# More buffers and longer leads for the half-precision parts of an attention and expert block

## The chip, the cores and the metric

The kernel runs on one core of one Trainium2 chip. The metric is the device time of one execution in microseconds (us), as the median of several runs. The core's engines are TensorE (PE, with its weight loads PEld), VectorE (DVE), ScalarE (ACT), GpSimd (POOL) and SyncE (SP). Nearly every DMA of this kernel is issued from SP, whose queue works in order: what waits there holds everything behind it.

## What is computed

```python
# x: 2048 tokens x 448 features
def _A_ref(x, wqkv, wo):                     # 16 heads of 28
    q, k, v = ...                            # of x @ wqkv
    p = softmax(q @ k.T * 28 ** -0.5)
    return (p @ v).reshape(...) @ wo

def _B_ref(x, w_q, k1, k2, u, v):            # 4096 experts in a 64 x 64 grid, 16 heads
    q1, q2 = halves of x @ w_q
    s1, s2 = q1 @ k1.T, q2 @ k2.T            # 64 scores each
    ...                                      # best 8 of each, best 8 of their 64 sums
    g = softmax(top_s)
    act = gelu(x . u[top_e])
    return sum(g * act * v[top_e])

h = x + _A_ref(layernorm(x), A_wqkv, A_wo)
return h + _B_ref(layernorm(h), B_w_q, B_k1, B_k2, B_u, B_v)
```

## The kernel before

A first part makes q, k and v, and stores them in DRAM. Then comes attention in 256 steps, called units here: one step is one block of 128 keys for four heads and 512 queries. It makes the scores S (line 526, PE), their exponentials P (line 530, ACT, two activations a step) and the sums A (line 552, PE). The keys and values are loaded again every four steps (`load_kv`, tiles `kS` and `V`). After every 64 steps a block of 512 tokens is done. `project` then turns it into the input of the second half: PE waits there for VectorE's `oh` and `xn`, VectorE for ScalarE. `search` scores the experts and picks the best eight. After attention, from about 1017 us on, the expert sums run; the change does not touch them.

All this is written out as generators, and `weave` puts their steps into one order: an entry (generator, n, lo, hi) spreads n steps over lo to hi, counted in attention steps. There are two weaves, one over steps 0 to 60 and one over the other 197, whose count starts again at 0. Within an engine the instructions stand in that order and run in it.

The expert tables u and v and the folded query weights are needed as half-precision parts: a table of fp32 rows is scaled and written as a high and a low fp16 plane (three planes for v). Three kinds of generators do it:

- `tops(S, ...)` loads a table once to find its largest magnitude; `S.see` is a VectorE reduction (line 139). It runs for u in the first weave (steps 1 to 25) and for v in the second (27 to 50).
- `S.share()` makes the scale from it, the same on all partitions.
- `part(S, src, dst, ...)` loads a block into a tile `raw`, makes the planes in a tile `hl`, and stores them in DRAM. For the folded weights (`parts_of_folded`, 16 parts, steps 5 to 27 of the second weave) VectorE makes them (lines 159 and 993), for u (`parts_of_up`, 14 parts in the first weave, 18 in steps 4 to 50 of the second) and for v (`parts_of_down`) GpSimd does (lines 988 to 990, and 995 for the third plane). `pipeline(..., 1)` starts one part per step, so that the steps of several parts overlap.

Before, a part loads in its first step, computes in its second and stores in its third. `raw` and `hl` have two buffers each, and the folded parts and those of u share them. `tops` has two buffers of 1024 columns of its own. A tile's instructions wait until the buffer that it takes has been read to the end by its last user; for `hl` this is the landing of the store.

Of the kernel before, what the change touches and what calls it, by code (L numbers as in the profile page):

```python
# [29 lines left out]
LS = 2.0 ** 11  # L30
# [28 lines left out]
def block(ctx: ExitStack, tc: tile.TileContext, x, wqk, wv, wo, wq, k12, uT, v, cst, out):  # L59
# [98 lines left out]
    def times(dst, src, c):  # L158
        nc.vector.tensor_scalar(dst, src, c, None, op0=OP.mult)  # L159
# [146 lines left out]
        STEPS = 3 * H  # L306


    US, VS, WS = Scale(0, 16), Scale(1, 16), Scale(2, H)

    fp = ExitStack()
    raw_p = fp.enter_context(tc.tile_pool(name="raw", bufs=2, reuse_waits="tile"))
# [285 lines left out]
    def project(b, offset=5, room=None):  # L598

        X[b] = XH, XL = bx.tile([128, 4, 512], F16, name="XHb"), bx.tile([128, 3, 512], F16, name="XLb")  # L600

        def place(j, name, tag, bufs):
            return room[name][j % len(room[name])] if room else w2.tile([128, 512], F32, name=name, tag=tag, bufs=bufs)

        def tile_of(j):
            r = 512 * b + 128 * j
            c = slice(128 * j, 128 * j + 128)
            xt = place(j, "xt", "xt", 2)[:, :D]
            nc.sync.dma_start(xt, x[r:r + 128])
            of = transposed(ob[b][:, j])  # L610
            oh = w2.tile([128, 4, 128], FR, name="oh2", bufs=1)
            ol = w2.tile([128, 3, 128], FR, name="ol2", bufs=1)
            if room:
                nc.scalar.activation(oh, of, AF.Copy)
            else:
                kept = w2.tile([128, 4, 128], F32, name="of", bufs=1)
                nc.scalar.activation(kept, of, AF.Copy)
                of = kept
            yield
            if not room:  # L620
                nc.vector.tensor_copy(oh, of)
            lows(oh, ol, of)
            yield
            if not room:
                yield
            pa = P[0].tile([128, 512], F32, name="M")
            mm_all(pa[:, :D], products(lambda t: oh[:, t], lambda t: ol[:, t], lambda t: woh[:, t], lambda t: wol[:, t]))
            at = place(j, "at", "xn", 1)[:, :D]
            nc.scalar.activation(at, pa[:, :D], AF.Copy)
            yield  # L630
            nc.vector.tensor_tensor(xt, at, xt, op=OP.add)
            nc.sync.dma_start(h_d[4 * b + j], xt)
            mean, rstd = moments(w2, xt)
            yield
            if not room:
                yield
            xn = w2.tile([128, 512], F32, name="xn2", tag="xn", bufs=1)[:, :D]
            norm(xt, xn, mean, rstd, nc.vector)
            if not room:
                yield  # L640
            xf = transposed(xn)
            if room:
                nc.scalar.activation(XH[:, :, c], xf, AF.Copy)
            else:
                kept = w2.tile([128, 4, 128], F32, name="xf", bufs=1)
                nc.scalar.activation(kept, xf, AF.Copy)
                xf = kept
            yield
            if not room:
                yield  # L650
                nc.vector.tensor_copy(XH[:, :, c], xf)
            lows(XH[:, :, c], XL[:, :, c], xf)
            yield

        yield from pipeline([tile_of(j) for j in range(4)], offset, -1 if room else 1)
        if not room:
            store_X(b)
# [310 lines left out]

    def tops(S, src, cols):

        raw = None
        for k in range(17):
            last = raw
            if k < 16:
                raw = sp.tile([128, 1024], F32, name="tops")
                nc.sync.dma_start(raw[:, :cols], src(2 * k))
            if last is not None:
                S.see(k - 1, last[:, :cols])
            yield

    def part(S, src, dst, cols, planes):
        raw = sp.tile([128, 512], F32, name="raw")
        nc.sync.dma_start(raw[:, :cols], src)
        yield
        hl = sp.tile([128, 3, 512], F16, name="hl")
        r, h = raw[:, :cols], [hl[:, k, :cols] for k in range(planes)]
        if planes == 3 or S is US:
            nc.gpsimd.tensor_scalar(r, r, S.scale, 1.0, op0=OP.mult, op1=OP.mult)
            nc.gpsimd.tensor_copy(h[0], r)
            nc.gpsimd.tensor_tensor(h[1], r, h[0], op=OP.subtract)  # L990
        else:
            times(h[0], r, S.scale)
            nc.vector.scalar_tensor_tensor(h[1], r, S.scale, h[0], op0=OP.mult, op1=OP.subtract)
        if planes == 3:
            nc.gpsimd.tensor_scalar(h[2], h[0], 1.0 / LS, 1.0, op0=OP.mult, op1=OP.mult)
        yield
        nc.sync.dma_start(dst, hl[:, :planes, :cols])
        yield

    def parts_of_up(f0, f1):  # L1000
        return pipeline([part(US, uT[:, f].rearrange("p t e -> p (t e)"), us_d[f], 512, 2) for f in range(f0, f1)], 1)
# [4 lines left out]
    def parts_of_folded():  # L1006
        return pipeline([part(WS, wr_d[h].rearrange("p t c -> p (t c)"),
                              wp_d[h // 4][:, :, h % 4].rearrange("p f t c -> p f (t c)"), 512, 2) for h in range(H)], 1)

    def scales():  # L1010
        times(ugelu, US.floor, 2.0 ** -TOP / XS)
        times(wscale, US.scale, 2.0 ** -17)
        nc.vector.tensor_tensor(oscale, US.floor, VS.floor, op=OP.mult)
        times(oscale, oscale, 2.0 ** -15)
        yield

    with tc.manual_schedule(engines={ET.PE, ET.DVE, ET.Activation, ET.Pool, ET.SP}):
        load_kv(2)
        start = [64 * b + 33 + PAIRED for b in range(3)]
        a = attention({u + 2 * n - 1 for u in start for n in range(16)})  # L1020
        weave((islice(a, 60), 60, 0, 60), (fold[0].run(fold_p, P[0]), Fold.STEPS, 1, 59),
              (tops(US, lambda f: uT[:, f:f + 2].rearrange("p f t e -> p (f t e)"), 1024), 17, 1, 25), (US.share(), 5, 26, 33),
              (parts_of_up(0, 14), 16, 33, 59))
        fp.close()
        bx = ctx.enter_context(tc.tile_pool(name="bx", bufs=1, reuse_waits="tile"))
        bg = ctx.enter_context(tc.tile_pool(name="bg", bufs=1, reuse_waits="tile"))
        bk = ctx.enter_context(tc.tile_pool(name="bk", bufs=1, reuse_waits="tile"))
        iota2 = bg.tile([128, 128, 2], F16)
        ident16 = bg.tile([128, 128], F16)
        sl = [bg.tile([128, 4, 128], F16, name=f"sl{j}") for j in range(4)]  # L1030
        ts4 = bg.tile([128, 4, H, 8], F32)
        for i in range(2):
            nc.vector.tensor_copy(iota2[:, :, i], ct[:, C_IOTA:C_IOTA + 128])
        nc.vector.tensor_copy(ident16, ident)
        places = pp.tile([128, 8, 16 * H], F16, name="places", bufs=1)
        for k in range(8):
            nc.gpsimd.memset(places[:, k], float(k))
        r2 = ExitStack()
        wo_p = r2.enter_context(tc.tile_pool(name="wo_p", bufs=1, reuse_waits="tile"))
        w2 = r2.enter_context(tc.tile_pool(name="w2", bufs=2, reuse_waits="tile"))  # L1040
        woh = wo_p.tile([128, 4, D], FR)
        wol = wo_p.tile([128, 4, D], FR)
        work = [(a, 197, 0, 197), (load_wo(), 5, 0, 8)]
        for b in range(3):
            t = 64 * b + 7
            look = search(b, [(i, j) for g in ((0, 1), (2, 3)) for i in range(4) for j in g])
            work += [(project(b), PROJECT, t, t + PROJECT), (islice(look, 1), 1, t + 10, t + 11)]
            t += 26
            work += [(look, SEARCH, t, t + SEARCH)]
            if b < 2:  # L1050
                work += [(chain(*[pairs_of(j, nc.gpsimd) for j in range(4)]), 4 * PAIRS_POOL, t + 18, t + 82),
                         (places_of(b, nc.scalar), PLACES, t + 82, t + 94)]
            else:
                work += [(pipeline([pairs_of(j, nc.gpsimd) for j in (0, 1)], 6), 6 + PAIRS_POOL, t + 20, 197)]
        work += [(WS.share(), 5, 0, 5), (parts_of_folded(), 18, 5, 27), (parts_of_up(14, 32), 20, 4, 50),
                 (tops(VS, lambda f: v[:, f:f + 2].rearrange("p f d -> p (f d)"), 2 * D), 17, 27, 50), (VS.share(), 5, 51, 56), (scales(), 1, 56, 57),
                 (parts_of_down(0, 14), 16, 58, 110), (parts_of_down(14, 32), 20, 110, 180)]
        weave(*work)
    att.close()
    late.close()  # L1060
# [176 lines left out]
```

## Time and profile before

| | before |
|---|---|
| time, median of 3 runs | 1780.12 us (1779.68 to 1780.82) |
| the profiled execution, its own time | 1786.24 us |
| its span, first to last instruction | 1784.4 us |
| mean granted TensorE clock | 0.958 |
| busy: PE, DVE, ACT, POOL | 90%, 70%, 50%, 23% |
| share of DMA: SP's queue q1 | 52.7% of 16 engines |

The span is 1.8 us shorter than the time of its own execution, and that execution is 6.1 us longer than the median of the others. In the rows of a window the columns are the window, its length, and for each engine its busy time with the number of instructions in brackets; then the granted TensorE clock, the busy share of the DMA engines and the GB/s that they moved. In the waits each row names who waited, for whom, the sum in us, how often and the longest.

### The profile page before, as it was taken

The page shows a single profiled execution, that of the slowest core. Times are in us where ns is not written, and L with a number is a line of the kernel's source. Part 1 is how long each engine was busy: PE and PEld are TensorE (multiplying, and loading weights), DVE is VectorE, ACT ScalarE, POOL GpSimd, SP SyncE. Part 2 cuts the span into 40 slices and gives each one's busy share as a digit, 9 for nine tenths or more (in the row PEclk, how much of TensorE's full clock was granted, in tenths as well). Part 3 has the DMA queues.
Part 4 walks back from the last instruction along what each step waited for, and adds up shares of the span by engine and source line. Part 5 has one row for each costly group of instructions (what it writes and reads, how often), then busy time and mean ns, then how long its engine had stood idle before and what let it go on. Part 6 is the DMA issues. An engine that isn't in the chain of part 4 may idle for free.

```text
span 1784.4 us, 33450 instructions
## 1 busy us (share of the span) xinstructions
PE 1608.8 (90%) x12577; PEld 816.0 (46%) x12577; DVE 1246.3 (70%) x3875; ACT 897.1 (50%) x1272; POOL 417.2 (23%) x514
## 2 busy tenths in 40 slices
PE   7999889953378999999999889899999999999998
PEld 5776334421133344334433356444554555455544
DVE  6655756422237956776767889995999899879932
ACT  3545566842156788768777534323342334433422
POOL 3452117511123167516743510000000000000000
PEclk9999999976689999999999899999999999999999
DMA  8756757544469556655665123444435543454344
GB/s 261 244 186 213 272 187 260 181 158 130 144 208 316 190 179 215 210 173 164 217 216 171 65 90 114 127 139 127 142 108 142 150 130 108 153 148 137 104 141 134
DMA packets 159748, 301.32 MB, mean 169 GB/s; under 512 B 14816, under 2 KB 58976, under 8 KB 159584
## 3 DMA queue, kind: packets, MB, share of 16 engines
q1 hardware_dynamic: 155360, 297.07, 52.7%
q8 instruction: 99, 1.62, 0.4%
q10 hardware_dynamic: 4224, 2.10, 0.4%
q14 instruction: 65, 0.53, 0.1%
HBM read 237.24 MB, written 61.87 MB: 168 GB/s over the span
## 4 chain that ended last, share of the span: by engine, by line
PE 54%; DVE 27%; DMA 12%; issue 2%; POOL 2%; SPq 1%; ACT 1%; DVEq 0%; POOLq 0%
PE acc L1152 13%; PE M L90 9%; PE A L552 8%; PE S L526 7%; PE A L90 7%; PE pq L90 6%; DVE p L932 4%; DVE ti L762 4%; DMA wp<-hl 3%; DMA tops<-in_v_dram 2%; DVE G L953 2%; DVE ti L761 2%; DVE fg L917 2%; DVE pos L789 2%; DMA us<-hl 1%
## 5 line engine op out<-in xcount | busy, mean ns | idle before, releaser
L530 ACT ACTIVATE P<-S 128x1024 f32<-128x1024 f32 x512 | 496.0, 1022 | 143.7 <-PE S L526 142.2
L1152 PE MATMUL acc<-v,w 128*128 128x448 f16 x1536 | 306.4, 353 | 0.7 <-DVE w L1127 0.7
L552 PE MATMUL A<-P,V 128*32 128x512 f32 x2048 | 272.5, 623 | 10.7 <-DVE o L557 10.7
L526 PE MATMUL S<-qS,kS 32*128 32x512 f32 x3072 | 269.0, 435 | 5.2 <-ACT P L530 4.6
L526 PEld LDWEIGHTS S<-qS,kS 32*128 32x128 f32 x3072 | 141.4, 188 | 164.1 <-issue 98.8
L1152 PEld LDWEIGHTS <-w 128*128 128x128 f16 x1536 | 148.7, 98 | 142.9 <-ACT w L1126 1.8
L90 PEld LDWEIGHTS <-u 128*128 128x128 f16 x1408 | 132.8, 98 | 149.2 <-issue 7.2
L1126 ACT ACTIVATE w<-ring 128x512 f16<-128x512 f32 x128 | 80.5, 630 | 209.2 <-PE acc L1152 109.8
L932 DVE TENSOR_TENSOR p<-st,iota 128x2048 f16<-128x2048 f16 x128 | 156.0, 1220 | 9.0 <-PE A L959 5.5
L90 PE MATMUL A<-XHb,u 128*128 128x512 f16 x568 | 135.4, 381 | 4.1 <-DVE G L953 4.0
L90 PE MATMUL M<-w,XHb 128*128 128x512 f16 x512 | 129.0, 382 | 6.9 <-DVE ob L543 3.7
L1127 DVE SCALAR_TENSOR_TENSOR w<-w,ring 128x512 f16<-128x512 f16 x128 | 87.2, 686 | 66.1 <-ACT w L1126 66.1
L1125 DVE SCALAR_TENSOR_TENSOR ring<-ring,wscale,G 128x512 f32<-128x512 f32 x128 | 92.8, 745 | 34.5 <-ACT ring L1111 34.5
L90 PE MATMUL M<-XHb,u 128*128 128x512 f16 x456 | 110.9, 379 | 0.8 <-DVE G L953 0.8
L552 PEld LDWEIGHTS A<-P,V 128*32 128x32 f32 x2048 | 46.3, 110 | 117.2 <-issue 101.0
L761 DVE MAX8 ti<-fresh 128x8 f32<-128x64 f32 x384 | 80.6, 210 | 16.9 <-ACT fresh L739 16.8
L1111 ACT ACTIVATE ring<-A,ugelu 128x512 f32<-128x512 f32 x71 | 48.5, 683 | 85.1 <-PE A L90 85.1
L813 POOL TENSOR_TENSOR sel<-sel,iv 128x256 f16<-128x256 f16 x80 | 54.2, 707 | 153.1 <-DVE sel L809 153.1
L159 DVE TENSOR_SCALAR hl<-raw,scale 128x512 f16<-128x512 f32 x16 | 7.8, 486 | 113.5 <-DMA wp<-hl 112.8
L762 DVE FIND_INDEX8 ti<-ti,fresh 128x8 uint32<-128x64 f32 x384 | 84.2, 219 | 0.0
L1111 ACT ACTIVATE ring<-M,ugelu 128x512 f32<-128x512 f32 x57 | 39.2, 688 | 81.7 <-PE M L90 81.5
L917 DVE TENSOR_TENSOR fg<-f,st 128x2048 f16<-128x2048 f16 x64 | 78.6, 1229 | 0.1
(197 smaller groups left out, 2360.9 us busy)
## 6 DMA issues: line engine op xcount, KB each, us to landing
v<-vs SPq DMA_DIRECT2D x128, 336.0 KB, 2.9
kS<-ks SPq DMA_DIRECT2D x64, 512.0 KB, 4.8
u<-us SPq DMA_DIRECT2D x128, 256.0 KB, 2.7
w<-wp SPq DMA_DIRECT2D x56, 512.0 KB, 5.4
V<-vd SPq DMA_DIRECT2D x64, 256.0 KB, 3.0
wr<-in_wq_dram SPq DMA_DIRECT2D x32, 448.0 KB, 6.1
vs<-hl SPq DMA_DIRECT2D x32, 336.0 KB, 4.0
qS<-qs SPq DMA_DIRECT2D x16, 512.0 KB, 5.8
```

The costliest lines, as they stand in the source:

```text
L90: nc.tensor.matmul(ps, l, r, start=i == 0, stop=i == len(pairs) - 1)
L526: nc.tensor.matmul(S[j // 2][:, j % 2], kS[r, a, 128 * (k % 4):128 * (k % 4) + 128], qS[r, c], start=m == 0, stop=m == 2)
L530: nc.scalar.activation(Pt[:, 2 * i:2 * i + 2], S[i], AF.Exp)
L552: nc.tensor.matmul(O[n][32 * j:32 * j + 32], V[:, k % 4, j], Pt[:, j], start=k == 0, stop=k == NT - 1)
L761: nc.vector.max(t8[:, 4 * i + k], src[:, 64 * k:64 * k + 64])
L762: nc.vector.max_index(i8[:, 4 * i + k], t8[:, 4 * i + k], src[:, 64 * k:64 * k + 64])
L917: nc.vector.tensor_tensor(fg.rearrange("p t k f u -> p t k (f u)"), f1.rearrange("p t f u -> p t (f u)").unsqueeze(2).to_broadcast([128, T ...
L932: newest[0] = nc.vector.tensor_tensor(p1, pairs(0, s, TG, 128), ids(TG, 128), op=OP.is_equal).ins
L1111: nc.scalar.activation(act, p, AF.Gelu_apprx_tanh, scale=ugelu)
L1125: nc.vector.scalar_tensor_tensor(av, av, wscale, of_expert(b, f), op0=OP.mult, op1=OP.mult)
L1127: nc.vector.scalar_tensor_tensor(w[:, 1], w[:, 0], -LS, a, op0=OP.mult, op1=OP.add)
L1152: nc.tensor.matmul(acc[j][:, :D], l, r, start=f == 0 and k == 0, stop=f == 31 and k == 2)
```

## The change

`tops` reads 32 blocks of 512 columns (448 for v) instead of 16 of 1024 (896), each loaded two steps of its generator ahead of its reduction instead of one; the weave gives it 34 steps instead of 17 in the same stretch. Its tiles are now the `raw` of the parts, of which there are six. A part computes two steps after its load and stores two steps after that. Parts of two planes have five buffers (`hl2`), parts of three planes three (`hl3`). The engines that make the planes stay the same. The first loads of `search` move 12 attention steps later, behind the last folded part.

```diff
-    US, VS, WS = Scale(0, 16), Scale(1, 16), Scale(2, H)
+    US, VS, WS = Scale(0, 32), Scale(1, 32), Scale(2, H)
...
     def tops(S, src, cols):
-        raw = None
-        for k in range(17):
-            last = raw
-            if k < 16:
-                raw = sp.tile([128, 1024], F32, name="tops")
-                nc.sync.dma_start(raw[:, :cols], src(2 * k))
-            if last is not None:
-                S.see(k - 1, last[:, :cols])
+        raw = {}
+        for k in range(34):
+            if k < 32:
+                raw[k] = sp.tile([128, 512], F32, name="raw", bufs=6)
+                nc.sync.dma_start(raw[k][:, :cols], src(k))
+            if k >= 2:
+                S.see(k - 2, raw.pop(k - 2)[:, :cols])
             yield
...
     def part(S, src, dst, cols, planes):
-        raw = sp.tile([128, 512], F32, name="raw")
+        raw = sp.tile([128, 512], F32, name="raw", bufs=6)
         nc.sync.dma_start(raw[:, :cols], src)
         yield
-        hl = sp.tile([128, 3, 512], F16, name="hl")
+        yield
+        hl = sp.tile([128, planes, 512], F16, name="hl", tag=f"hl{planes}", bufs=5 if planes == 2 else 3)
...
         yield
-        nc.sync.dma_start(dst, hl[:, :planes, :cols])
+        yield
+        nc.sync.dma_start(dst, hl[:, :, :cols])
         yield
+    PART = 4
...
-              (tops(US, ...), 17, 1, 25), (US.share(), 5, 26, 33),
-              (parts_of_up(0, 14), 16, 33, 59))
+              (tops(US, ...), TOPS, 1, 25), (US.share(), 5, 26, 33),
+              (parts_of_up(0, 14), 14 + PART, 33, 59))
...
-            work += [(project(b), PROJECT, t, t + PROJECT), (islice(look, 1), 1, t + 10, t + 11)]
+            work += [(project(b), PROJECT, t, t + PROJECT), (islice(look, 1), 1, t + 22, t + 23)]
...
-        work += [(WS.share(), 5, 0, 5), (parts_of_folded(), 18, 5, 27), (parts_of_up(14, 32), 20, 4, 50),
-                 (tops(VS, ...), 17, 27, 50), ...
-                 (parts_of_down(0, 14), 16, 58, 110), (parts_of_down(14, 32), 20, 110, 180)]
+        work += [(WS.share(), 5, 0, 5), (parts_of_folded(), H + PART, 5, 27), (parts_of_up(14, 32), 18 + PART, 4, 50),
+                 (tops(VS, ...), TOPS, 27, 50), ...
+                 (parts_of_down(0, 14), 14 + PART, 58, 110), (parts_of_down(14, 32), 18 + PART, 110, 180)]
```

The order on PE and on ACT stays as it was, instruction for instruction. On SP it changes in the stretch of the two passes and of the parts. At the start of the folded parts (second weave, steps 6 to 13) SP's queue stood so before; `wp` is the DRAM tensor of the folded parts, `us` that of u, `wr` the folded weights, and the numbers tell the tiles apart:

```order
L983 DMA raw_27690<-wr2_68 128x512
L997 DMA wp0_82<-hl_27687 256x1x512
L983 DMA raw_27720<-wr3_69 128x512
L997 DMA us14_120<-hl_27642 128x1024
L983 DMA raw_27748<-in_uT_dram 128x512
L997 DMA wp0_82<-hl_27717 256x1x512
L983 DMA raw_27789<-wr4_70 128x512
```

Now it stands so, at the same place:

```order
L984 DMA raw_27730<-wr2_68 128x512
L984 DMA raw_27759<-wr3_69 128x512
L984 DMA raw_27765<-in_uT_dram 128x512
L1000 DMA wp0_82<-hl_27727 256x1x512
L984 DMA raw_27792<-wr4_70 128x512
L1000 DMA wp0_82<-hl_27756 256x1x512
L984 DMA raw_27833<-wr5_71 128x512
```

The store of the first folded part (`hl_27727`) has moved behind the loads of the third and fourth; two parts of each table are loaded beyond the one that is stored. On SP in the first weave, where the pass over u begins, the rows were these (`wr` is here the raw query weight for the fold):

```order
L201 DMA qS<-qs_58 128x2x512
L976 DMA tops<-in_uT_dram 128x1024
L242 DMA wr<-in_wq_dram 128x896 x2
L976 DMA tops<-in_uT_dram 128x1024
L201 DMA kS<-ks_61 128x2x512
```

And they are now:

```order
L201 DMA qS<-qs_58 128x2x512
L975 DMA raw<-in_uT_dram 128x512 x3
L242 DMA wr<-in_wq_dram 128x896 x2
L975 DMA raw<-in_uT_dram 128x512
L201 DMA kS<-ks_61 128x2x512
```

One load of 1024 columns has become up to three of 512 ahead of the same neighbours.

More of the change, by code (lines that the diff above doesn't have):

```diff
@@ L969, in tops @@
     def tops(S, src, cols):
-        raw = None
-        for k in range(17):
-            last = raw
-            if k < 16:
-                raw = sp.tile([128, 1024], F32, name="tops")
-                nc.sync.dma_start(raw[:, :cols], src(2 * k))
-            if last is not None:
-                S.see(k - 1, last[:, :cols])
+        raw = {}
[5 more added lines that the diff above has]
+                S.see(k - 2, raw.pop(k - 2)[:, :cols])
             yield
+    TOPS = 34
     def part(S, src, dst, cols, planes):
-        raw = sp.tile([128, 512], F32, name="raw")
+        raw = sp.tile([128, 512], F32, name="raw", bufs=6)
         nc.sync.dma_start(raw[:, :cols], src)
         yield
-        hl = sp.tile([128, 3, 512], F16, name="hl")
+        yield
+        hl = sp.tile([128, planes, 512], F16, name="hl", tag=f"hl{planes}", bufs=5 if planes == 2 else 3)
         r, h = raw[:, :cols], [hl[:, k, :cols] for k in range(planes)]
-        if planes == 3 or S is US:
+        if S is WS:
+            times(h[0], r, S.scale)
+            nc.vector.scalar_tensor_tensor(h[1], r, S.scale, h[0], op0=OP.mult, op1=OP.subtract)
+        else:
             nc.gpsimd.tensor_scalar(r, r, S.scale, 1.0, op0=OP.mult, op1=OP.mult)
@@ L990, in part @@
             nc.gpsimd.tensor_tensor(h[1], r, h[0], op=OP.subtract)
[L991 to L995, printed above, removed]
+            if planes == 3:
+                nc.gpsimd.tensor_scalar(h[2], h[0], 1.0 / LS, 1.0, op0=OP.mult, op1=OP.mult)
         yield
-        nc.sync.dma_start(dst, hl[:, :planes, :cols])
         yield
+        nc.sync.dma_start(dst, hl[:, :, :cols])
+        yield
+    PART = 4
     def parts_of_up(f0, f1):
@@ L1021, in block @@
         weave((islice(a, 60), 60, 0, 60), (fold[0].run(fold_p, P[0]), Fold.STEPS, 1, 59),
-              (tops(US, lambda f: uT[:, f:f + 2].rearrange("p f t e -> p (f t e)"), 1024), 17, 1, 25), (US.share(), 5, 26, 33),
-              (parts_of_up(0, 14), 16, 33, 59))
+              (tops(US, lambda f: uT[:, f].rearrange("p t e -> p (t e)"), 512), TOPS, 1, 25), (US.share(), 5, 26, 33),
+              (parts_of_up(0, 14), 14 + PART, 33, 59))
         fp.close()
@@ L1054, in block @@
                 work += [(pipeline([pairs_of(j, nc.gpsimd) for j in (0, 1)], 6), 6 + PAIRS_POOL, t + 20, 197)]
-        work += [(WS.share(), 5, 0, 5), (parts_of_folded(), 18, 5, 27), (parts_of_up(14, 32), 20, 4, 50),
-                 (tops(VS, lambda f: v[:, f:f + 2].rearrange("p f d -> p (f d)"), 2 * D), 17, 27, 50), (VS.share(), 5, 51, 56), (scales(), 1, 56, 57),
-                 (parts_of_down(0, 14), 16, 58, 110), (parts_of_down(14, 32), 20, 110, 180)]
+        work += [(WS.share(), 5, 0, 5), (parts_of_folded(), H + PART, 5, 27), (parts_of_up(14, 32), 18 + PART, 4, 50),
+                 (tops(VS, lambda f: v[:, f], D), TOPS, 27, 50), (VS.share(), 5, 51, 56), (scales(), 1, 56, 57),
+                 (parts_of_down(0, 14), 14 + PART, 58, 110), (parts_of_down(14, 32), 18 + PART, 110, 180)]
         weave(*work)
```

## The prediction

> **What bounds the kernel now.** I first read the page's slices, to find where PE, which is busy 90% of the span, is not.
>
> ```profile
> PE   7999889953378999999999889899999999999998
> ```
>
> Slices 9 to 12 (357 to 535 us; a slice is 44.6 us) hold 5, 3, 3 and 7 tenths. Second come the windows around that hole, first those of all engines, then the exponentials alone (line 530, two per attention step).
>
> ```profile
> 154.50:197.10 42.60, 41.11 (x352) 17.85 (x354) 30.40 (x40) 32.50 (x35) 8.43 (x4) 0.96 0.75 262
> 197.10:246.20 49.10, 37.71 (x288) 16.49 (x284) 31.08 (x42) 24.84 (x27) 6.30 (x3) 0.86 0.68 226
> 356.40:520.20 163.80, 75.09 (x568) 35.01 (x571) 40.41 (x81) 53.06 (x61) 30.65 (x40) 0.70 0.46 144
> 520.20:563.50 43.30, 38.50 (x303) 14.48 (x303) 24.37 (x99) 26.23 (x29) 12.33 (x15) 0.93 0.93 320
> 644.60:708.20 63.60, 63.27 (x568) 29.54 (x571) 40.55 (x130) 52.64 (x60) 42.05 (x59) 1.00 0.62 199
> 708.20:744.70 36.50, 35.55 (x303) 13.99 (x304) 26.30 (x149) 26.26 (x30) 18.70 (x26) 1.00 0.73 233
> 540.00:550.00 10.00, 9.27 (x63) 3.29 (x67) 7.28 (x39) 3.81 (x5) 2.50 (x4) 0.83 1.01 376
> ```
>
> ```profile
> 154.50:197.10 42.60, 31.03 (x32) 0.96 0.75 262
> 197.10:246.20 49.10, 23.26 (x24) 0.86 0.68 226
> 356.40:520.20 163.80, 46.43 (x49) 0.70 0.46 144
> 644.60:708.20 63.60, 46.43 (x48) 1.00 0.62 199
> ```
>
> The kernel contains its own control. 356.4:520.2 and 644.6:708.2 are the same 24 attention steps of two blocks, with the same 568 matmuls and the same `project`. The first takes 163.8 us, the second 63.6 with PE busy for 63.27. What the first has more is the folded parts and those of u. Third, the waits in that window (the last row is SP's own queue):
>
> ```profile
> DVE hl L159 <- DMA wp<-hl: 112.8, 15, 16.4
> POOL hl L989 <- DMA us<-hl: 84.2, 8, 14.4
> PEld M L119 <- DVE xn L113: 60.0, 3, 26.5
> SPq L983 <- DVE hl L993: 53.0, 12, 9.1
> ```
>
> VectorE stands 112.8 us before making a folded part until the store of an earlier part has landed; PE stands 60 us for `project`'s `xn`, which is queued behind that on VectorE. Fourth, the chain of waits shows the loop:
>
> ```profile
> 407.73 3.26 DMA wp<-hl
> ...
> 411.12 0.50 DVE hl L159
> ...
> 411.64 0.76 DVE hl L993
> ...
> 412.42 0.33 SPq L983
> ...
> 412.79 3.07 DMA wp<-hl
> ```
>
> A store lands (3.1 to 3.3 us), VectorE makes the planes (0.50 + 0.76), SP, which waited for the raw buffer, issues a load (0.33), only then the next store, and so on: 4.9 us a part, strictly in series, because two `hl` and two `raw` serve both tables. Sixteen folded parts make 78 us of it, and ten parts of u of the same build the rest.
>
> In the first weave there is a smaller hole. Steps 0 to 16 take 42.6 us, 2.66 a step; the next twelve 49.1, 4.09 a step:
>
> ```profile
> 201.14 1.22 DVE L139 TENSOR_REDUCE tops<-tops 128x1 f32<-128x1024 f32 x1 [4.09 <-DMA tops<-in_uT_dram]
> ...
> 206.07 0.71 PE L90 MATMUL M<-wqh,kk 128*128 128x448 f32 x1 [5.16 <-DVE wt L267]
> 221.21 0.44 PE L90 MATMUL M<-wqh,kk 128*128 128x448 f32 x1 [1.15 <-DVE wt L267]
> 234.57 0.71 PE L90 MATMUL M<-wqh,kk 128*128 128x448 f32 x1 [4.96 <-DVE wt L267]
> ```
>
> VectorE waits for a block of u that could not be loaded earlier for want of a third buffer, and PE's fold waits behind it.
>
> **The change part by part.**
>
> *The parts in the second weave.* In steps of the weave, a folded part computes every 22/20 = 1.1 steps, one of u every 46/22 = 2.1. In the built program each compute now takes a buffer whose store stands up to two steps earlier in SP's order (before: in the same step, just ahead), and that store's data were made two or four steps before, so SP need not wait for it. A cycle of three folded parts needs some 1.26 + 0.33 + 3.3 = 4.9 us against 3.3 steps of 2.65 (63.6/24) = 8.7. So the loop opens. What is late next?
>
> - PE: 63.6 us, the twin window.
> - DMA: the bytes stay. The busy share of 0.46 over 163.8 us is 75.3 us of DMA time. The fullest stretch of the table, 520.2:563.5, reached 0.93, so 75.3/0.93 = 81.0 us. This is more than PE's 63.6, so DMA is the next bound.
> - Waits that stay. Four folded parts late in the stretch take a buffer of u whose store stands in SP's order in the same step as their compute. If SP is not ahead, each costs VectorE a store issue and landing, 0.33 + 3.3 us and what SP still has ahead of it, some 4.5: 0 to 18 us in all. I take 8, near the middle, since a stall of VectorE also leaves DMA idle.
>
> So 163.8 becomes 81 + 8 = 89, a gain of 75. The bounds: 100 if PE alone binds, 44 in the second rival below.
>
> *The pass over u.* Its loads may now run up to six reductions ahead instead of two, 1.5 MB instead of 1 MB in flight. I take back the three PE stalls shown: 5.16 + 1.15 + 4.96 = 11.3 us. At best the twelve steps go at 2.66 us, 49.1 - 31.9 = 17.2 (the clock of 0.86 recovers too); at worst nothing. DMA in 154.5:246.2 is 0.75 x 42.6 + 0.68 x 49.1 = 65.3 us busy and does not bind the 80.4 us that are left.
>
> *The pass over v* (second weave, steps 27 to 50). Its lead in bytes hardly changes, the DMA share is at 0.93 there, and its bytes are the same. Its twin 708.2:744.7 takes 36.5 us against 43.3, so 0 to 6.8 are to be won; I take 0.
>
> *More, smaller operations.*
>
> ```profile
> L139 DVE TENSOR_REDUCE tops<-tops 128x1 f32<-128x1024 f32 x16 | 19.3, 1208 | 11.4 <-DMA tops<-in_uT_dram 11.4
> L139 DVE TENSOR_REDUCE tops<-tops 128x1 f32<-128x896 f32 x16 | 17.2, 1078 | 24.0 <-DMA tops<-in_v_dram 24.0
> L139 DVE TENSOR_REDUCE tops<-of 128x1 f32<-128x512 f32 x16 | 10.9, 682 | 23.2 <-ACT of L279 23.2
> ```
>
> 32 reductions of 512 at 0.682 are 21.8 us for 19.3; 32 of 448, about 0.60, 19.1 for 17.2: 4.4 us more on VectorE, and 32 more issues of 0.33 are 10.6 us on SP. VectorE is busy 61 of 92 us and 24 of 43 in these stretches, so I take 0; without that cover it is up to 15.
>
> *Queues passed.* The loads now stand ahead of `kS` and `V` loads that were ahead of them, and six of the v blocks ahead of the GpSimd operation that frees their buffer. SP can stand there up to 2.5 us each, 0 to 15. The keys behind are loaded eight steps (over 20 us) before they are used; I take 0. The stores two steps later have no near reader: `search` reads the folded parts, and its first loads move with them. These are three transfers, now four steps (10.6 us) ahead of the search, which needs two of them first.
>
> ```profile
> tops<-in_uT_dram SPq DMA_DIRECT2D x16, 512.0 KB, 5.1
> raw<-in_uT_dram SPq DMA_DIRECT2D x32, 256.0 KB, 4.3
> tops<-in_v_dram SPq DMA_DIRECT2D x16, 448.0 KB, 5.7
> raw<-in_v_dram SPq DMA_DIRECT2D x32, 224.0 KB, 4.2
> w<-wp SPq DMA_DIRECT2D x56, 512.0 KB, 5.4
> ```
>
> Two `w` at 5.4 just fit if they come one after the other; in three blocks a late one may cost some us each, 0 to 15 in all. I take 0. The parts of v, with three buffers of their own, lie in windows where PE is already busy to 99% (63.27 of 63.60): 0.
>
> *Sum.* 75 + 11.3 = 86 off the span of 1784.4 gives 1698; the execution's own 1786.2 becomes 1700. It stood 6.1 above the median of the runs, 1780.1, so the median should be **1694 us**.
>
> **The rivals.**
>
> *DMA doesn't bind.* [...] 144 GB/s x 163.8 us are 23.6 MB; in 63.6 us that is 371 GB/s, and one stretch of 10 us reached 376. Then PE binds: 100.2 + 17.2 gained, 1663. Against it: 376 held for 10 us only, and with a share of 1.01. "Perfetto Trace Analysis" of the Trainium skill (section Roofline) lets a single core reach about 435 GB/s over its 16 DMA engines; by that these bytes would take an estimated 54 us, and this rival would be the forecast. The row of 376 at a full share speaks against counting on it. Chance 0.10.
>
> *The change does only part of what it says: the buffers still tie the two tables.* SP can't run ahead, because it waits for folded stores and `xt` of the same steps, and every folded part still waits for one issue and landing, 0.33 + 3.2 = 3.5 us, on VectorE: 16 x 3.5 = 56 on top of 63.6 is 120 us, a gain of 44. With the 11.3 of the pass over u this gives 1725. For it: five buffers for two tables is few. Chance 0.14.
>
> *Slower: the halved loads go one at a time.* A load of half the size lands hardly sooner, 4.3 for 5.1 and 4.2 for 5.7. If SP stops between them, at a `V` whose buffer PE still reads or at a `raw` that a part still holds, so that fewer than two blocks are in flight, the pass over u needs 32 x 4.3 = 138 us instead of 91.7 (+46), and that over v 32 x 4.2 = 134 instead of some 83 (23 steps at 43.3/12; +51). Less the 75 of the parts this is +22: 1802. With two or more in flight it is harmless. Against it stand the six buffers and the 0.33 us of an issue. Chance 0.05. The Trainium skill, "DMA: Bandwidth & Descriptors", section Rules for kernel authors, speaks against the change in the same way: many small transfers are to be coalesced, and full bandwidth wants 1 MiB per DMA. By it the halving alone would slow both passes; the rows above agree that a half load saves only 0.8 to 1.5 us, but here the loads can overlap.
>
> *No change that can be measured*, the gain eaten by all the small terms at once: 0.01.
>
> **How the numbers follow.** My forecast, 1675 to 1715 around 1694, gets 0.70; the rivals 0.10, 0.14, 0.05 and 0.01. The range 1670 to 1730 holds the forecast, most of the partial case and the edge of the fast one, and leaves out under 0.2. A measurement of this kernel tells 0.2% (3.6 us) from no change. Faster: 0.70 + 0.10 + 0.14 = 0.94; same 0.01; slower 0.05.
>
> **What would show it.** Right: 24 attention steps after about 345 us in 80 to 100 us, VectorE's wait for `wp<-hl` down from 112.8 to under 20, DMA share there over 0.8, PE's clock back near 1, no PE wait of 5 us in the pass over u. Wrong: VectorE still waiting for `wp<-hl` by 40 us or more, a DMA share at 0.5, or SP waiting long for GpSimd in front of raw loads, with PE waiting for `V` or `kS`.

## The result, and the profile after

The changed kernel takes 1703.43 us in the median of four runs (1696.69 to 1704.53), beside 1780.47 for the kernel before on the same chip: a ratio of 0.9554, with an interval of 0.9525 to 0.9584, or 77.0 us less. (The ratios here are worked out from all runs; the two medians alone would give 0.9567.) The profiled execution of it took 1696.69 us with a span of 1694.9. That is 89.5 us below the span of before, more than the medians differ, since this execution is 6.7 us under its own median and the profiled one of before was 6.1 over its. Only profiled executions have stages, so stages are compared with stages below, and times with times.

The page's slices of PE and of its granted clock have lost the hole (a slice is 42.4 us here):

```profile
PE   6999898987899999999998899899999999999999
PEclk9999999998999999999999999999999999999999
```

These are the windows of all engines. The first two are steps 0 to 16 and 16 to 28 of the first weave, the third is the 24 steps with the folded parts, the fourth the twelve steps behind, and the last the twin of the third. Steps are counted here, and below wherever a step number goes with a measured stretch, from the start of attention through both weaves; so the 24 steps are 68 to 92, the twelve behind them 92 to 104, and the twin 132 to 156. Only the places to which parts of u are moved below (30 to 120 and the like) are counted as in the weave's table, within the second weave:

```profile
153.30:198.60 45.30, 41.15 (x353) 17.82 (x354) 30.49 (x48) 32.58 (x35) 8.46 (x4) 0.96 0.78 250
198.60:240.90 42.30, 35.49 (x288) 15.64 (x288) 31.38 (x50) 24.74 (x28) 6.31 (x3) 0.92 0.77 257
349.60:432.20 82.60, 68.32 (x568) 31.44 (x572) 50.01 (x83) 53.02 (x61) 36.95 (x44) 0.92 0.85 281
432.20:473.50 41.30, 37.02 (x303) 14.45 (x299) 24.21 (x107) 26.23 (x30) 14.81 (x18) 0.96 0.98 345
554.90:619.60 64.70, 63.38 (x568) 29.61 (x572) 41.35 (x130) 52.66 (x60) 41.33 (x59) 1.00 0.60 181
```

The 24 steps went from 163.8 to 82.6 us: 81.2 of the 89.5. Steps 0 to 28 of the first weave together gave 4.1 (91.7 to 87.6), the twelve steps after the folded parts 2.0, and all the rest 2.2. These are the waits in the 24 steps:

```profile
DVE hl L159 <- DMA us<-hl: 14.5, 4, 5.0
DVE hl L159 <- DMA wp<-hl: 5.9, 2, 4.3
PEld M L119 <- DVE xn L113: 8.1, 2, 5.4
```

VectorE's 112.8 us for `wp<-hl` are 5.9, and PE's 60.0 for `xn` are 8.1. The longest wait is a new one: four times VectorE stands for the store of a part of u. The chain of waits shows one of them:

```profile
386.69 4.86 DMA us<-hl
...
391.68 0.72 DVE hl L159
...
393.09 0.51 DVE xn L113
...
397.79 4.63 DMA wp<-hl
402.41 0.49 DVE hl L159
```

The folded part waits for the buffer of u, `xn` is queued behind it on VectorE, and PE waits for `xn`, as before, but no longer at every part. In the 24 steps PE itself stands five times, always for VectorE, 14.3 us in all: 9.7 us of it (4.45, 1.69 and 3.54) come after the first and the third of the four stalls, while PE works on through the second and the last (3.11 and 4.38).

### The profile page after: what moved, and what is told of

It reads as the page before. It is cut to its first block, busy times and chain, and to the rows that moved or that the text cites. A ratio compares the mean times of both kernels' runs of the same rounds, so it can differ in the third digit from the quotient of the medians.

```text
span 1694.9 us, 33544 instructions
## 1 busy us (share of the span) xinstructions
PE 1598.7 (94%) x12577; PEld 811.4 (48%) x12577; DVE 1254.8 (74%) x3907; ACT 896.7 (53%) x1272; POOL 421.1 (25%) x514
## 4 chain that ended last, share of the span: by engine, by line
PE 62%; DVE 24%; DMA 8%; issue 2%; POOL 1%; ACT 1%; SPq 0%; DVEq 0%; POOLq 0%; ACTq 0%
PE acc L1157 15%; PE M L90 10%; PE A L90 9%; PE A L552 9%; PE S L526 9%; PE pq L90 6%; DVE p L932 4%; DVE ti L762 2%; DVE G L953 2%; DMA raw<-in_uT_dram 2%; DVE fg L917 2%; DVE pos L789 2%; DMA raw<-in_v_dram 1%; DVE ti L761 1%; PE A L959 1%
## 5 line engine op out<-in xcount | busy, mean ns | idle before, releaser
L552 PE MATMUL A<-P,V 128*32 128x512 f32 x2048 | 267.8, 613 | 3.4 <-DVE o L557 3.4
L90 PEld LDWEIGHTS <-XHb 128*128 128x128 f16 x512 | 45.4, 98 | 72.5 <-issue 21.3
```

Source lines behind the costliest of these rows:

```text
L90: nc.tensor.matmul(ps, l, r, start=i == 0, stop=i == len(pairs) - 1)
L552: nc.tensor.matmul(O[n][32 * j:32 * j + 32], V[:, k % 4, j], Pt[:, j], start=k == 0, stop=k == NT - 1)
```

## The experiments

**Which half of the change?** The passes were put back (with five `raw` buffers and narrower tiles for three planes, so that all fits), and then the passes were changed alone, with six buffers of their own.

```diff
# e1_parts_alone: the changed kernel, passes as before
-  raw = sp.tile([128, 512], F32, name="raw", bufs=6)
+  raw = sp.tile([128, 512], F32, name="raw", bufs=5)
+  # tops(), Scale(0, 16), Scale(1, 16), 17 steps as before
# e2_pass_alone: the kernel before, with
+  # tops() of 32 blocks, two ahead
+  raw[k] = sp.tile([128, 512], F32, name="tops", bufs=6)
```

> The parts as changed (leads of two steps, five buffers for two planes), the passes as before (two buffers of 1024 columns, one step ahead; raw has five buffers here, since six do not fit beside them). If the hole was the loop of store, planes and load on two shared buffers, this alone gives nearly all: the 24 attention steps of the first block in 80 to 90 us (163.8 before, 82.6 changed), a time of 1703 to 1715. If the deeper loads of the passes carry a good part of the gain, it stays above 1725.

> The passes as changed (32 blocks of 512 columns, two ahead, six buffers of their own), the parts as before. If the gain is the parts', the first block keeps its 160 us or so and the time falls by 4 to 12 us, to 1768 to 1776, by the first 28 attention steps alone (91.7 us before, 87.6 changed). If halved loads hurt, it is 1785 or more.

The parts alone took 1708.8 us, a ratio of 0.9593 (0.9558 to 0.9627). The passes alone took 1780.53 beside 1781.36, a ratio of 0.9995 (0.9977 to 1.0012). So the parts carry nearly all of the gain, and the passes none that can be measured; the 4 to 12 us that were expected of them did not come. The windows of the 24 steps and VectorE's largest wait there, first of the parts alone, then of the passes alone:

```profile
352.10:436.60 84.50, 70.90 (x568) 32.60 (x572) 44.32 (x81) 52.92 (x60) 35.70 (x43) 0.88 0.83 267
...
DVE hl L159 <- DMA us<-hl: 21.3, 6, 5.5
```

```profile
350.10:514.70 164.60, 77.38 (x568) 36.47 (x572) 41.05 (x82) 53.08 (x60) 30.57 (x40) 0.70 0.47 143
...
DVE hl L159 <- DMA wp<-hl: 113.8, 15, 16.5
```

**Which of the two buffers?** Each was given to the kernel before, alone.

```diff
# e8_raw6: the kernel before, with
-        raw = sp.tile([128, 512], F32, name="raw")
+        raw = sp.tile([128, 512], F32, name="raw", bufs=6)
# e9_hl5: the kernel before, with
-        hl = sp.tile([128, 3, 512], F16, name="hl")
+        hl = sp.tile([128, 3, 512], F16, name="hl", bufs=5)
```

> The kernel before with one edit: six raw buffers for the parts. In the loop SP waits at each raw load for the planes of the part before, and only then issues the store. If the raw buffers close the loop, this alone brings the first block from 163.8 us to 85 to 110 us and the time to 1705 to 1730. If the planes' buffers do, VectorE waits for wp<-hl as long as before (over 80 us), the block stays over 140 us and the time over 1755.

> The kernel before with the other edit alone: five buffers for the planes. If the planes' buffers close the loop, the block goes to 85 to 110 us and the time to 1705 to 1730, with no wait for wp<-hl left. If the raw buffers do as well, SP still waits for planes at each raw load, VectorE now for raw<-wr instead of wp<-hl, the block stays over 120 us and the time over 1735.

They took 1718.97 and 1718.29 us, ratios of 0.964 (0.9614 to 0.9666) and 0.964 (0.9615 to 0.9665): either alone gives four fifths of what the change gives (3.6% of 4.5%). The 24 steps of `raw` alone and of `hl` alone, each with VectorE's largest wait:

```profile
353.30:453.10 99.80, 71.46 (x568) 33.13 (x572) 43.97 (x81) 53.05 (x61) 30.62 (x40) 0.86 0.73 234
...
DVE hl L159 <- DMA wp<-hl: 36.8, 12, 8.9
```

```profile
353.20:450.20 97.00, 72.47 (x568) 33.02 (x572) 42.75 (x81) 52.97 (x60) 31.93 (x40) 0.84 0.75 241
...
DVE hl L159 <- DMA raw<-wr: 45.0, 13, 7.4
```

The loop of the prediction ran through both buffers: a store's landing frees `hl`, the making of planes frees `raw`, and a load refills it, with one SP queue between them. Taking either buffer out of it opens it. What is left is a wait of VectorE for a landing at most of the 16 parts: that of a store where `hl` stays at two (36.8/12 = 3.1 us in the mean), that of a load where `raw` does (45.0/13 = 3.5 us).

**Are the longer leads needed?** The buffers were kept, and a part was given its old steps.

```diff
# e3_old_leads: the changed kernel, part() with
         nc.sync.dma_start(raw[:, :cols], src)
         yield
-        yield
         hl = ...
         ...
         yield
-        yield
         nc.sync.dma_start(dst, hl[:, :, :cols])
-    PART = 4
+    PART = 2
```

> All as changed, but a part computes one step after its load and stores one step after that, as before: only the buffers are more. If the buffers alone break the loop, the first block takes 80 to 95 us and the time is 1700 to 1715. If the leads are needed too (SP waiting at each store for planes just made, VectorE at each part for a load just issued), it takes 100 to 135 us and the time is 1720 to 1755, with VectorE waiting for raw<-wr and SP for hl.

It took 1703.57 us, a ratio of 0.9568 (0.9537 to 0.9599): no different from the whole change. In the windows of the 24 and the next twelve steps and in VectorE's waits one loss stands for another:

```profile
353.30:432.70 79.40, 70.05 (x570) 32.61 (x572) 48.66 (x82) 52.99 (x60) 34.18 (x40) 0.89 0.84 275
432.70:479.00 46.30, 38.82 (x303) 14.86 (x301) 24.72 (x108) 26.28 (x30) 13.05 (x16) 0.93 0.94 333
...
DVE hl L159 <- DMA raw<-wr: 20.3, 7, 4.5
```

The store of u is no longer waited for, since it stands earlier in SP's order; the load of the folded part is, since it has one step less. The 24 steps are 3.2 us shorter, the next twelve 5.0 longer.

**Does DMA bind what is left?** The prediction held DMA to be the next bound at 81 us. If so, more buffers can't help.

```diff
# e4_hl7: the changed kernel, with
-  bufs=5 if planes == 2 else 3
+  bufs=7 if planes == 2 else 3
```

> All as changed, with seven buffers instead of five for parts of two planes. If the four waits of VectorE for us<-hl (14.5 us) and what PE loses behind them are what holds the first block at 82.6 us, they go and it takes 66 to 74 us; time 1688 to 1696. If DMA binds there, as the prediction's 81.0 us had it, the waits go but the block stays at 79 to 83 us, VectorE or PE waiting for loads instead, and the time stays within 4 us of the changed kernel.

It took 1691.78 us, a ratio of 0.9511 (0.9473 to 0.955). The interval overlaps that of the change, but the stage is clear. Here are its window and what is left of VectorE's wait:

```profile
351.70:426.20 74.50, 66.64 (x568) 30.15 (x572) 52.42 (x83) 52.82 (x61) 38.67 (x43) 0.95 0.92 311
...
DVE hl L159 <- DMA raw<-wr: 5.8, 4, 2.2
```

VectorE waits for no store any more, and the same bytes went in 74.5 us. DMA did not bind at 81 or at 82.6: the four waits for the buffer cost the stage some 8 us (82.6 - 74.5). What holds it at 74.5, with a DMA share of 0.92 and PE idle for 7.9 us, is not shown.

**What held the pass over u?** In both profiles SP itself stands in steps 0 to 28 of the first weave. Of SP's own queue, before and after:

```profile
SPq L213 <- PE A L552: 25.2, 6, 7.2
SPq L976 <- DVE tops L139: 12.4, 9, 3.8
```

```profile
SPq L213 <- PE A L552: 24.6, 6, 8.5
```

Line 213 loads `V`, which has three buffers; SP waits there until PE has read the oldest, and the loads of the pass stand behind it. A fourth buffer of `V` was given to the kernel before, and to the kernel with the passes alone.

```diff
# e13_before_v4, e14_pass_v4: the kernel before, and that of e2_pass_alone, with
-  V = lp.tile([128, 4, 4, 32], F32, name="V", bufs=3)
+  V = lp.tile([128, 4, 4, 32], F32, name="V", bufs=4)
```

> The kernel before with four V buffers instead of three, and nothing else. If SP's stop at V is what starves the pass over u, and not the pass's own two buffers, this alone shortens the first weave by 6 to 12 us: time 1769 to 1776. If the pass's two buffers bind as the prediction had it, it stays within 3 us of the kernel before.

> The same with the passes as changed (32 blocks of 512 columns, two ahead, six buffers of their own), the parts as before. If both bind one after the other, the changed passes now show what V hid, and this is 4 to 10 us faster than four V buffers alone. If the passes never bound, it is the same within 3 us.

They took 1768.57 and 1769.05 us, ratios of 0.9931 (0.9908 to 0.9954) and 0.9929 (0.9905 to 0.9952): 13.7 us for one buffer, and the changed passes add nothing to the time even then. The same 87 us of the first weave, in the kernel before, with the fourth buffer, and with the fourth buffer and the changed passes:

```profile
154.00:241.00 87.00, 74.12 (x600) 32.18 (x596) 58.62 (x78) 53.14 (x58) 14.72 (x7) 0.90 0.72 247
```

```profile
154.00:241.00 87.00, 79.74 (x686) 34.82 (x686) 65.06 (x89) 61.74 (x68) 16.86 (x8) 0.98 0.79 271
```

```profile
154.00:241.00 87.00, 77.58 (x640) 33.91 (x641) 62.88 (x101) 57.97 (x64) 14.77 (x7) 0.94 0.77 259
```

With the fourth buffer PE does 686 matmuls in place of 600, and SP's row for line 213 is gone from that stretch; with the changed passes as well it does 640. So by these profiles `V` held the old pass, but it is not all that holds the new one. Steps 0 to 28 took 91.7 us before, 81.5 with four `V`, 85.4 with the changed passes, and 86.3 with both. The largest wait of SP's queue from 153 to 246 us is then at line 283, the store of a folded weight that waits for ScalarE's `of`. Here is that row, before and with both:

```profile
SPq L283 <- ACT of L279: 17.0, 5, 5.0
```

```profile
SPq L283 <- ACT of L279: 38.7, 7, 9.0
```

Part of what SP no longer waits at `V` it waits there; what the pass itself could win stays open. Nor is the time that the fourth buffer won the pass's alone: steps 28 to 60, in which the first parts of u are made, took 92.6 to 96.3 us in the nine profiles with three buffers and 89.6 to 91.3 in the five with four.

**Where should the parts of u stand?** The 18 late parts of u share the 24 steps with the folded parts only by the weave's table. They were moved: over steps 30 to 120; with four buffers of `V`, to 34 to 70; and with four buffers of `V`, in three groups that keep clear of the `project` of each block. The fourth kernel joins seven `hl2` with four `V` (and narrower tiles for three planes, to fit).

```diff
# e10_u_later: the changed kernel, with
-  (parts_of_up(14, 32), 18 + PART, 4, 50)
+  (parts_of_up(14, 32), 18 + PART, 30, 120)
# e12_v4_u_late: V bufs=4 and
+  (parts_of_up(14, 32), 18 + PART, 34, 70)
# e11_v4_u_three: V bufs=4 and
+  (parts_of_up(14, 20), 6 + PART, 40, 64), (parts_of_up(20, 26), 6 + PART, 98, 128),
+  (parts_of_up(26, 32), 6 + PART, 162, 192)
# e7_hl7_v4: V bufs=4 and hl2 bufs=7
```

> All as changed, five buffers, but the second weave's parts of u run over attention steps 30 to 120 instead of 4 to 50, so that nearly all come after the folded parts; nothing needs them before the expert sums. Some 5 of 23 MB leave the first block, and no folded part takes a buffer of u. If contention between the two tables (buffers or DMA) holds the first block at 82.6 us, it falls to 64 to 70 us, the next twelve steps from 41.3 to 36 to 40 us, and the time to 1680 to 1690. If project's own chain through VectorE holds it, it stays over 76 us and the time over 1695. If GpSimd's part of the pair search suffers from the parts beside it, the later blocks grow by what the first one wins.

> The same with the parts of u in one stretch, steps 34 to 70, ahead of the second block's project but beside the pass over v. DMA was at a share of 0.98 beside that pass. If DMA binds there, the first block gains as in the other run but steps 92 to 132 (122.7 us in the changed kernel) stay at 121 us or more; if not, they fall to 118 or less. Time 1674 to 1684.

> All as changed, five buffers, with four V buffers, and the second weave's parts of u cut in three groups of six that lie in searches instead of projects: steps 40 to 64, 98 to 128 and 162 to 192. If contention between the two tables was what the first block still paid (69.7 us with u later, 63.7 in its twin) and the growth of the second block in the run before (64.7 to 68.4 us) came from u's parts beside its project on GpSimd, the first block takes 66 to 70, the next twelve steps 36 to 39, the second block 63.5 to 65, and with the 4 us or more of the V buffers the time is 1672 to 1680. If the second block grew for another reason it stays at 68 and the time is 1678 to 1686.

> All as changed, with seven buffers for parts of two planes and four instead of three for the V of attention (parts of three planes have tiles of 448 columns to make room). SP stood 24.6 us at V loads during the pass over u in the changed kernel, with the pass's loads behind it. If that is why the pass still makes VectorE wait for its loads, the first 28 attention steps fall from 88 to 78 us and the time to 1678 to 1684. If DMA is simply slow there, they stay at 85 to 89 us and the time is that of seven buffers alone, 1688 to 1696.

| kernel | us, median | ratio (interval) | the 24 steps | next twelve |
|---|---|---|---|---|
| after | 1703.43 | 0.9554 (0.9525 to 0.9584) | 82.6 | 41.3 |
| e10_u_later | 1690.30 | 0.9488 (0.9463 to 0.9512) | 69.7 | 38.3 |
| e7_hl7_v4 | 1682.29 | 0.9435 (0.9408 to 0.9462) | 72.6 | 40.7 |
| e12_v4_u_late | 1675.44 | 0.9394 (0.9367 to 0.9422) | 67.7 | 39.5 |
| e11_v4_u_three | 1674.67 | 0.9390 (0.9349 to 0.9431) | 68.5 | 37.6 |

The two stages in the table are from one profile each. Moving u's parts alone (`e10_u_later`) is worth 13.1 us; the kernels below it in the table have the fourth `V` buffer as well. Seven `hl2` with four `V` reached the expected time, but not by the expected stage: steps 0 to 28 fell from 88.0 us with seven `hl2` to 84.7, not to 78.

Without u's parts the 24 steps come within 4 to 6 us of the 63.6 of the twin in the kernel before. Moving them has a price where they land. In the kernel with u over steps 30 to 120, the 24 steps of the twin took 68.4 us and not 64.7; with the three groups they took 64.7 again, so u's parts beside the second `project` made that difference. With u at 34 to 70, steps 104 to 132 took 88.0 us in its profile and not 81.4: PE does the same 686 matmuls, at a granted clock of 0.96 in place of 1.00, and has one long wait that the changed kernel has not, for a load of the folded parts (`w`):

```profile
PE M L90 <- DMA w<-wp: 3.1, 1, 3.1
```

What made that load late is not shown; steps 92 to 132 took 127.5 us, which was to be the sign of DMA as the bound, but at a DMA share of 0.82 in steps 104 to 132 that is not shown either. That execution took 1682.88 us, 7.4 over its kernel's median, and the times of that kernel and of the three groups do not differ, so this price is seen in one profile only. The three groups are the best version that was run, 28.8 us below the changed kernel.

## Why the prediction was right, point by point

**The hole and its cause: right.** The loop of landing, planes and load on two shared buffers was what made 24 steps last 163.8 us. Parts alone, `raw` alone and `hl` alone all open it, and the passes alone leave it at 164.6. The stage was forecast at 89 and took 82.6; the waits for `wp<-hl` are under 20, as foretold, and the DMA share is over 0.8. The clock came back only to 0.92 there. The prediction's sum for the loop was not complete: 26 parts at 4.9 us are 127 us, not 163.8. For u the planes are made by GpSimd, and SP stood 39.1 us in eight waits for them (`SPq L983 <- POOL hl L990`), a row that the prediction did not use.

**The four waits that stay: right.** They were to be four folded parts that wait for the store of u, 0 to 18 us. The profile shows exactly four, with 14.5 us. Of these the stage paid 8.1, what seven `hl2` took off it; the 8 that I took was the middle of a range and not worked out, so its closeness is luck.

**"DMA is the next bound", 81.0 us: wrong.** 74.5 us with seven buffers rules it out. The failed step is 0.46 x 163.8 = 75.3 us of DMA time taken as fixed and divided by 0.93. The busy share of the same work was 0.85 x 82.6 = 70.2 us in the changed kernel and 0.92 x 74.5 = 68.5 with seven buffers. By bytes, with the rate of the same row that gave the 0.93, the step would have been 23.6 MB/320 GB/s = 73.7 us. What made up the 18 us over the twin in its place is PE's idle time, 82.6 - 68.3 = 14.3 against 1.3 in the twin, and a clock of 0.92 (68.3 us of matmuls for 63.4). The stage's miss, 89 for 82.6, is this one term: 81.0 stood where seven buffers gave 74.5.

**The pass over u, 11.3 us: mis-sized; it is nothing that the times show.** The step that failed is "could not be loaded earlier for want of a third buffer". The three PE stalls stand at the same places, in steps 17, 21 and 24, in all four kernels with the old passes and three `V` (before, parts alone, `raw` alone, `hl` alone): 11.3 us together before, 8.6 to 8.8 in the others. With six buffers they are 6.3 us in the changed kernel; with two buffers and a fourth `V` they are 5.1. So the third buffer was not what they wanted most. And with the new passes PE waits three times in steps 6 to 13 where it had not waited, 0.70, 1.11 and 0.95 us in the changed kernel. Steps 16 to 28 took 43.2 to 49.1 us in those four kernels and 40.9 to 43.2 in five with the new passes and three `V` (after, passes alone, old leads, seven `hl2`, u later); steps 0 to 16 took 42.5 to 43.5 and 43.5 to 49.2. One change is set off by the other: steps 0 to 28 took 88.8 and 88.0 us in the mean. Here is the work in the changed kernel, with VectorE's wait and PE's in those steps:

```profile
DVE tops L139 <- DMA raw<-in_uT_dram: 9.0, 7, 3.1
PE M L90 <- DVE wt L267: 7.9, 5, 3.0
```

So "no PE wait of 5 us" came true and was worth nothing. SP's stand at `V`, 25.2 and 24.6 us, was in the trace of before; the prediction names a stop at `V` in its third rival only, and the forecast gives it no price. What makes VectorE late in steps 6 to 13 is not shown; the loads that now pass others in SP's queue, taken at 0, may be part of it.

**The rest.** The pass over v at 0: right (the twelve steps took 41.3 us, and 42.5 to 44.1 in the three kernels with other buffers and the old passes). The smaller operations at 0: right; 32 reductions cost 21.3 us as forecast, beside other work:

```profile
L139 DVE TENSOR_REDUCE tops<-raw 128x1 f32<-128x512 f32 x32 | 21.3, 676 | 9.0 <-DMA raw<-in_uT_dram 9.0
```

The later first loads of `search` at 0: right, steps 104 to 132 took 81.1 us before and 81.4 after.

**The rivals.** *DMA doesn't bind* was right that 81 us is no bound and wrong about this kernel: the buffers still held it, and it takes seven of them, or u's parts elsewhere, to come nearer to PE's time. Whether DMA can carry the 371 GB/s that the rival needs through the whole stage is not shown; the fastest stage above moved 345. *The buffers still tie the tables* was a third right: 14.5 + 5.9 = 20.4 us of such waits in place of its 56. *The halved loads go one at a time* fell: the passes alone are at 0.9995. The rule of the Trainium skill that stands behind it ("DMA: Bandwidth & Descriptors", Rules for kernel authors: coalesce small transfers) made no difference to the time here, from 512 KB to 256 KB a load.

**The sum.** 86 us were forecast and 77.0 measured: 75 for the block, which gave 81.2 between the profiled executions, and 11.3 for the pass, which gave nothing that the times show. The two misses have opposite signs, and that they partly cancel is luck. How much of the block's 81.2 belongs to these two executions alone stays open, since the medians have no stages; the parts alone moved the median by 72.6.

## What to carry to other kernels

Where two pipelines share a pool of two buffers, look for the loop landing, compute, load in the chain of waits: more buffers on either side of it (here five or six for two) bring most of the gain, and what is left shows which side to widen next. Before a missing buffer is blamed for a late load, read what the issuing queue itself waits for over the same stretch: here a `V` that PE had not read yet held back every load behind it, and one buffer there was worth 13.7 us, a whole new scheme for the loads nothing that could be measured. Look at the queue again after that: the next wait in it may take over. Bound a stage's DMA by its bytes and the best rate that another stage reached, not by its busy time: here that gives 73.7 us in place of 81.0, beside 74.5 measured.

## What the hardware showed

DMA busy time per byte fell as the rate rose. The 24 steps move 23.1 to 23.6 MB in the kernel before, the changed one and that with seven `hl2`; the DMA engines were busy for 75.3 us of it at 144 GB/s, 70.2 at 281 and 68.5 at 311. A single transfer takes longer meanwhile. These are the DMA issues in the 24 steps, before and then after, with the median from issue to landing at the end of each row:

```profile
raw<-wr SPq DMA_DIRECT2D x16, 256.0 KB, 2.9
wp<-hl SPq DMA_DIRECT2D x16, 256.0 KB, 3.2
```

```profile
raw<-wr SPq DMA_DIRECT2D x16, 256.0 KB, 5.1
wp<-hl SPq DMA_DIRECT2D x16, 256.0 KB, 4.6
```

So a wait for a landing, priced from a stage at 144 GB/s, is too cheap for the same stage at 281: 2.9 and 3.2 us became 5.1 and 4.6. And the granted clock went with PE's idle time: the 568 matmuls of the 24 steps cost 75.09 us of PE at 0.70, 68.32 at 0.92 and 63.38 at 1.00, so a stall costs more than its own length. The Trainium skill tells of this ("TensorE: Matmul & The Clock Gate", Part 1): the clock is throttled by default, and sustained activity releases it. These three rows agree.
